# Activation differences of the last 1024 tokens, weight sums and first loads, taken elsewhere in a two-MLP kernel

## The chip, the cores and the metric

The kernel runs on one core of a Trainium2 chip. The metric is the device time in microseconds (us); each version is timed in several runs and the median counts. A core has five engines that run side by side, each working through its own list of instructions in order: TensorE (PE in the profile; matrix products, its weight loads shown as PEld), VectorE (DVE), ScalarE (ACT), GpSimd (POOL) and SyncE (SP), which here only issues DMAs between DRAM and the on-chip memory. An instruction waits for semaphores of the instructions that it depends on, and everything behind it on its engine waits with it.

## The reference

A retention layer, then two MLPs with the same sizes: 3072 tokens, 512 features, 2048 hidden features.

```python
for t in range(S):          # S = 768, 4 batches, 8 heads of 64
    state = gamma * state + outer(k[:, :, t], v[:, :, t])
    y[:, :, t] = scale * q[:, :, t] @ state
x = y.transpose(0, 2, 1, 3).reshape(3072, 512)
h = x @ w_in;   x = (h * cos(h)) @ w_out                       # first MLP, layer 0
h = x @ w_in2;  out = where(h > 0, h, exp(min(h, 0)) - 1) @ w_out2   # second MLP, layer 1
```

## The kernel before

**Number format.** TensorE works on fp32r. Each operand is split into a high part (written by ACT) and a low part (the rest, formed on DVE by a subtraction of two on-chip operands), and each product is the sum of three matmul terms, high-high, high-low, low-high (`PARTS`). A weight tile `w` of a slice holds seven operands of 256 columns in both parts.

**Seven products.** Three of the four MLP products are made as 2 by 2 block products with seven instead of eight multiplications. The weight operands are three blocks of the slice (`a11`, `a12`, `a22`) and four sums (`s1` to `s4`, made of the blocks and of `a21`). The activation operands are four quarters `x0, x1, y0, y1` of a superblock (512 tokens each) and three differences. `A_OF` and `B_OF` name the operands of product `p`; products run in the order 1, 5, 6, 3, 7, 2, 4.

**Stages, in the order in which TensorE runs them** (times of the profile):
- 0 to 31 us: four 128-token units of the retention layer (`scores`, `values`, `update` for unit `n`), with a few dummy matmuls (`warm`). A unit's 1 MB of inputs is one DMA (`load_unit`); `scale_unit` then multiplies q and v by decay factors.
- 31 to 381.7 us, "hidden": `hidden(blk, j)`, the first product of layer 0 without the seven-product form, for six blocks of 512 tokens and eight weight slices `j`, the other 20 units between them. After it come the cosine factor and, for the first two superblocks, the differences (`pair_up`); those of the third are made later, in the next stage (`pair_up_late`, eight times, called from `first_pairs`).
- 381.7 to 614.6 us, "project(0)": `project(0, sb)`, the second product of layer 0 for three superblocks `sb` of 1024 tokens. Each of the 7 x 4 pairs of a superblock is 12 matmuls (line 822) and needs one activation tile `hl`, split by ACT and DVE.
- 614.6 to 890.5 us, "hidden2": the first product of layer 1, 24 steps of (superblock, slice). Step names here are as 2.7 (superblock 2, slice 7). One product is six matmuls (line 628). Steps overlap: `seven(new, old)` interleaves products 1, 5, 6, 3 of the new step with 7, 2, 4 of the old one. Between them DVE must add a saved partial sum to what TensorE has just summed (for instance line 679, between product 7 and product 4 of a step, which sum into the same bank). Then comes the ELU (`elu`: ACT, and DVE lines 724, 733, 736), four subtractions of 128x512 (`differences`) and four stores to DRAM (`put`). At a superblock's first step the seven tiles of the next input (`load_x2`) are loaded and split.
- 890.5 to 1137 us, "project(1)": `project(1, sb)`, the second product of layer 1, with its transposes and stores (`emit`).

**Weights.** They arrive as 8-byte floats. `convert` turns a slice into fp32, forms the four sums (four 128x256 operations), and stores the seven operands to DRAM in two DMAs (three and four operands). `prepare`, called shortly before the slice is needed, loads them back in two DMAs and splits them (ACT, then DVE line 393). `convert` of the slices for project(0) and hidden2 is called in hidden, `prepare` at the end of hidden and in project(0); for the slices of project(1), `convert` is called in hidden2's first two superblocks and `prepare` in its last.

**What sets the order.** The program first lists its operations (`Plan`). TensorE's order is the order of the list. For the other engines `Plan.run` makes the order by list scheduling: a due time for each operation, worked out backwards from TensorE's order and from assumed durations, and then always the ready operation that is due first. An operation marked `ANY` goes to DVE or POOL, whichever comes free first; one that overlaps another on the port is assumed to take `CROWDED` times as long, and a DMA to land after `LANDING`. Buffers come from small pools (11 `c`, 5 `h`, 4 `hl`, 3 `ld`, 8 `w`, 3 `eg`); an operation whose buffer is not free is put off. The outcome is a fixed order of instructions on each engine.

Of the kernel before, what the change touches and what calls it, by code (L numbers as in the profile page):

```python
# [259 lines left out]
def retention_then_two_mlps(ctx: ExitStack, tc: tile.TileContext, attn, tab, weights, out):  # L260
# [117 lines left out]
    def prepare(layer, io, j, lag=0):  # L378
        k = kept[layer, io][j]
        w = Buf("w", [P, NP, 2, Q], F32R)  # L380
        w_t[layer, io, j] = w
        for lo, hi in ((0, 3), (3, NP)):
            t = Buf("c", [P, hi - lo, Q])
            dma(
                hi - lo, lambda t=t: t.t.rearrange("p n q -> p (n q)"),
                lambda lo=lo, hi=hi: k.t[:, lo * Q:hi * Q], [k[lo * Q, hi * Q]], [t], lag,
            )
            high = lambda lo=lo, hi=hi: w.t[:, lo:hi, 0, :]

            turn = -1.0 if layer == 0 else 1.0  # L390
            act(0.1 + 0.26 * (hi - lo), high, lambda t=t: t.t, [t], [w[lo, hi]], lag=lag, scale=turn)
            plan.op("DVE", 0.08 + 0.29 * (hi - lo), lambda t=t, lo=lo, hi=hi, high=high:
                    nc.vector.scalar_tensor_tensor(  # L393
                        out=w.t[:, lo:hi, 1, :], in0=t.t, scalar=turn, in1=high().bitcast(F32),
                        op0=ALU.mult, op1=ALU.subtract,
                    ), [t, w[lo, hi]], [w[lo, hi]], lag)
# [138 lines left out]
    def differences(x, y, u, t4, t4_at, wid, lag):  # L535
# [4 lines left out]
        for o, a, b in todo:  # L540
            tt("ANY", (0.62, 1.2), view(o), view(a), view(b), ALU.subtract, [a, b], [o], lag=lag)


    def hidden(blk, j):
# [40 lines left out]
        else:  # L585
            pair_up(sb, j, g, u, 30)

    def pair_up(sb, j, g, u, lag):
# [4 lines left out]
        put(0, sb, j, 0, 2, lambda: g.t, [g], lag)
        put(0, sb, j, 4, 6, lambda: u.t, [u], lag)
        put(0, sb, j, 6, 7, lambda: t4.t, [t4], lag)

    def pair_up_late(sb, j, lag):
# [430 lines left out]
```

## Time and profile before

| | |
|---|---|
| median of 3 runs | 1138.35 us (1137.36 to 1138.43) |
| the profiled execution | 1138.94 us, its span 1137.2 us |
| TensorE busy | 1081.7 us, 95% of the span |
| DVE, ACT, POOL busy | 858.1, 619.9, 376.2 us |
| DMA | 329.57 MB, 290 GB/s in the mean |

The page gives totals. Three views tell more. The windows give, for chosen stretches, the busy time of each engine, the granted clock of TensorE as a share of full speed (PEclk) and the share of time in which the DMA engines were busy. The waits list whom an engine waited for; a wait below 0.15 us isn't counted. The timeline shows single instructions, with the idle time before an instruction, and what ended it, in square brackets. Six matmuls in one timeline row are one product of hidden2.

### The profile page before, as it was taken

The numbers are of one execution on the slowest core, as the hardware profiler recorded it, in microseconds if no ns is written. First come the engines' busy times: TensorE is split into PE (matmuls) and PEld (weight loads), VectorE is DVE, ScalarE is ACT, GpSimd is POOL, SyncE is SP. The second block draws the span as 40 slices with busy tenths as digits, with TensorE's granted clock in tenths as the row PEclk, the third lists the DMA queues.
The fourth block names the chain that finished last, engine by engine and source line by source line (L and its number), as shares of the span: only waits on it lengthen the run. The fifth ranks groups of instructions, "written<-read, shape, count | busy, mean of one in ns | idle before, by whom it ended". The sixth has DMA issues, their size and how long they took to land. (4 is left out here: it accounts for less than half of the span.)

```text
span 1137.2 us, 14708 instructions
## 1 busy us (share of the span) xinstructions
PE 1081.7 (95%) x5382; PEld 880.8 (77%) x5384; DVE 858.1 (75%) x896; ACT 619.9 (55%) x719; POOL 376.2 (33%) x288
## 2 busy tenths in 40 slices
PE   6999999999999999999998999998988799999997
PEld 4777888888788888877787777776767688888886
DVE  5998999899988847665568898898787845445452
ACT  3564455544567853433446867666677543444442
POOL 2413664466613023222102455675365400000000
PEclk9999999999999999999999999999989899999999
DMA  8776799989999998999998878968878876667661
GB/s 318 288 232 246 274 328 351 340 321 329 341 327 351 328 326 297 354 327 328 338 371 311 301 256 322 335 261 316 291 294 307 296 254 225 218 197 229 203 203 56
DMA packets 117289, 329.57 MB, mean 290 GB/s; under 512 B 8929, under 2 KB 15201, under 8 KB 114273
## 3 DMA queue, kind: packets, MB, share of 16 engines
q1 hardware_dynamic: 117216, 328.64, 81.4%
q8 instruction: 42, 0.69, 0.3%
q14 instruction: 31, 0.25, 0.1%
HBM read 197.01 MB, written 131.60 MB: 289 GB/s over the span
## 5 line engine op out<-in xcount | busy, mean ns | idle before, releaser
L822 PE MATMUL eg<-hl,w 128*128 128x512 f32 x2016 | 465.7, 391 | 2.9 <-DVE hl L293 2.8
L822 PEld LDWEIGHTS eg<-hl,w 128*128 128x128 f32 x2016 | 376.9, 188 | 82.8 <-DVE hl L293 5.0
L293 POOL TENSOR_TENSOR c<-c 128x512 f32<-128x512 f32 (+2 forms) x204 | 283.7, 1398 | 393.0 <-DVE c L293 94.7
L293 DVE TENSOR_TENSOR hl<-ld,hl 128x1024 fp32r<-128x1024 f32 x168 | 218.4, 1313 | 131.3 <-ACT hl L288 131.2
L288 ACT ACTIVATE hl<-ld 128x1024 fp32r<-128x1024 f32 x168 | 176.4, 1059 | 239.4 <-PE eg L822 175.0
L288 ACT ACTIVATE c<-c 128x1024 f32<-128x1024 f32 (+1 forms) x256 | 231.4, 921 | 98.5 <-DVE c L573 65.0
L556 PE MATMUL eg<-hl,w 128*128 128x512 f32 x1152 | 273.9, 394 | 4.4 <-DVE c L578 2.5
L556 PEld LDWEIGHTS eg<-hl,w 128*128 128x128 f32 x1152 | 213.0, 188 | 54.4 <-issue 4.8
L628 PE MATMUL eg<-hl,w 128*128 128x512 f32 x432 | 116.2, 404 | 26.3 <-DVE c L293 22.1
L288 ACT ACTIVATE c<-eg 128x1024 int32<-128x1024 f32 (+2 forms) x96 | 87.5, 911 | 73.5 <-PE eg L556 47.5
L628 PEld LDWEIGHTS eg<-hl,w 128*128 128x128 f32 x432 | 81.4, 193 | 52.0 <-DVE c L293 29.2
L293 DVE TENSOR_TENSOR c<-c 128x512 f32<-128x512 f32 (+2 forms) x72 | 61.4, 854 | 32.5 <-DMA c<-d 21.4
L628 PE MATMUL eg<-ld,w 128*128 128x512 f32 x288 | 74.2, 392 | 3.0 <-ACT h L288 2.9
L293 POOL TENSOR_TENSOR ld<-ld,w 128x512 f32<-128x512 f32 x34 | 47.6, 1414 | 62.5 <-DMA ld<-in_attn 52.5
L628 PEld LDWEIGHTS eg<-ld,w 128*128 128x128 f32 x288 | 54.5, 190 | 15.3 <-ACT h L288 3.3
L393 DVE SCALAR_TENSOR_TENSOR w<-c,w 128x768 fp32r<-128x768 f32 (+1 forms) x48 | 65.4, 1384 | 1.1 <-ACT w L288 1.0
L578 DVE SCALAR_TENSOR_TENSOR c<-c,eg 128x1024 f32<-128x1024 f32 x48 | 58.4, 1216 | 9.1 <-ACT c L288 8.8
L573 DVE SCALAR_TENSOR_TENSOR c<-eg,c 128x1024 f32<-128x1024 f32 x48 | 58.3, 1215 | 5.2 <-ACT c L288 4.6
L288 ACT ACTIVATE w<-c 128x1024 fp32r<-128x1024 f32 (+3 forms) x59 | 52.6, 918 | 16.3 <-DMA c<-d 9.3
L323 DVE SCALAR_TENSOR_TENSOR c<-c 128x512 uint32<-128x512 uint32 x64 | 58.4, 928 | 1.0
L327 DVE SCALAR_TENSOR_TENSOR c<-c 128x512 uint32<-128x512 uint32 x64 | 54.6, 870 | 0.4
L293 DVE TENSOR_TENSOR c<-eg,h 128x512 f32<-128x512 f32 x48 | 32.9, 685 | 19.2 <-PE eg L628 17.9
(50 smaller groups left out, 778.2 us busy)
## 6 DMA issues: line engine op xcount, KB each, us to landing
d<-c SPq DMA_DIRECT2D x197, 512.0 KB, 4.4
ld<-d SPq DMA_DIRECT2D x84, 1024.0 KB, 7.3
c<-d SPq DMA_DIRECT2D x77, 512.0 KB, 5.5
c<-in_weights SPq DMA_DIRECT2D x64, 512.0 KB, 6.1
ld<-in_attn SPq DMA_DIRECT2D x23, 1024.0 KB, 6.8
d<-c SPq DMA_DIRECT2D x24, 384.0 KB, 3.5
c<-d SPq DMA_DIRECT2D x24, 384.0 KB, 5.2
d<-h SPq DMA_DIRECT2D x24, 256.0 KB, 6.9
```

Source lines behind the costliest of these rows:

```text
L288: plan.op("ACT", us, lambda: nc.scalar.activation(out=out_(), in_=in_(), func=func, **kw), r, w, lag)
L293: e.tensor_tensor(out=out_(), in0=a(), in1=b(), op=op)
L323: plan.op("DVE", 0.69, lambda: nc.vector.scalar_tensor_tensor(out=u(), in0=raw.t[:, :, 1], scalar=0x80000000, in1=u(), op0=ALU.bitwise_and ...
L327: plan.op("DVE", 0.69, lambda: nc.vector.scalar_tensor_tensor(out=u(), in0=raw.t[:, :, 0], scalar=29, in1=u(), op0=ALU.logical_shift_right ...
L393: nc.vector.scalar_tensor_tensor(out=w.t[:, lo:hi, 1, :], in0=t.t, scalar=turn, in1=high().bitcast(F32), op0=ALU.mult, op1=ALU.subtract,), ...
L556: nc.tensor.matmul(out=h.t[:, half * TB:(half + 1) * TB], lhsT=quarter(j, qd, wpart, kc % 2), rhs=(xh, xl)[xpart].t[:, kc, :], start=(n == ...
L573: plan.op("DVE", 1.22, lambda: nc.vector.scalar_tensor_tensor(out=g.t, in0=h.t, scalar=1.0 / TWO_PI, in1=n(), op0=ALU.mult, op1=ALU.subtra ...
L578: plan.op("DVE", 1.22, lambda: nc.vector.scalar_tensor_tensor(out=g.t, in0=g.t, scalar=1.0, in1=h.t, op0=ALU.subtract, op1=ALU.mult,), [h, ...
L628: nc.tensor.matmul(out=out_(), lhsT=w.t[:, i, wpart, kc * P:(kc + 1) * P], rhs=x.t[:, xpart, kc, :], start=(start and n == 0), stop=(n == ...
L822: nc.tensor.matmul(out=acc.t[:, i * TB:(i + 1) * TB], lhsT=w[:, A_OF[p], wpart, i * P:(i + 1) * P], rhs=hl.t[:, gpart, k, :], start=(p in ...
```

## The change

Four things change.
1. For superblock 2 of layer 1 (`LATE = 2`), `seven` no longer makes the differences nor stores them. It stores the two activation tiles alone. In project(1), `second_pairs` calls `pair_up_late(1, 2, j)` at two of the four places `jp` of each product of superblock 1, until the eight slices are done: it loads both tiles again, makes the four subtractions and stores what changed.
2. `convert` stores the four blocks of a slice in one DMA and forms no sums. `prepare` loads them in one DMA, forms the four sums itself and splits blocks and sums.
3. Units 1 to 3 are loaded in three DMAs each (`EARLY`) instead of one.
4. Three of the planner's numbers change: `CROWDED`, `LANDING`, and the time assumed for a 128x512 operation on POOL (1.2 to 1.25).

```diff
-CROWDED = 1.4
-LANDING = 2.8
+LATE = 2
+CROWDED = 1.6
+LANDING = 3.0
 ...
     def convert(layer, io, j, lag):
         t = to_f32(layer, io, j, lag)
-        s = Buf("c", [P, WS])
 ...
-        dma(3, lambda: k.t[:, 0:3 * Q], lambda: t.t[:, 0:3 * Q], [t[0, 3 * Q]], [k[0, 3 * Q]], lag)
-        dma(4, lambda: k.t[:, 3 * Q:], lambda: s.t, [s], [k[3 * Q, NP * Q]], lag)
+        k = kept[layer, io][j]
+        dma(4, lambda: k.t, lambda: t.t, [t], [k], lag)
+
+    def prepare(layer, io, j, lag=0):
 ...
+        t, s = Buf("c", [P, WS]), Buf("c", [P, WS])
+        dma(4, lambda: t.t, lambda: k.t, [k], [t], lag)
+        def split(src, at, lo, hi):
 ...
+        split(t, t[0, 3 * Q], 0, 3)
         a11, a12, a22, a21 = ((t, q * Q, q * Q + Q) for q in range(4))
         s1, s2, s3, s4 = ((s, q * Q, q * Q + Q) for q in range(4))
 ...
             tt("ANY", (0.35, 0.7), view(o), view(a), view(b), op, [a, b], [o], lag=lag)
+        split(s, s, 3, NP)
 ...
-            differences(old.x, old.y, old.ux, old.uy, 0, TB, lag)
+            if old.sb < LATE:
+                differences(old.x, old.y, old.ux, old.uy, 0, TB, lag)
             put(1, old.sb, old.j, 2, 4, lambda: old.y.t, [old.y], lag)
             put(1, old.sb, old.j, 0, 2, lambda: old.x.t, [old.x], lag)
-            put(1, old.sb, old.j, 4, 6, lambda: old.ux.t, [old.ux], lag)
-            put(1, old.sb, old.j, 6, 7, lambda: old.uy.t[:, 0:TB], [old.uy[0, TB]], lag)
+            if old.sb < LATE:
+                put(1, old.sb, old.j, 4, 6, lambda: old.ux.t, [old.ux], lag)
+                put(1, old.sb, old.j, 6, 7, lambda: old.uy.t[:, 0:TB], [old.uy[0, TB]], lag)
 ...
+    EARLY = ((0, 1024), (1024, 1536), (1536, 2048))
 ...
-    load_unit(1)
+    load_unit(1, EARLY)
 ...
+    last = [(sb, j) for sb in range(LATE, NSB) for j in range(NJ)]
+    def second_pairs(sb, p, jp):
+        if jp % 3 == 0 and last and last[0][0] == sb + 1:
+            pair_up_late(1, *last.pop(0), 60)
     for sb in range(NSB):
-        project(1, sb, lambda *_: None)
+        project(1, sb, second_pairs)
```

**The order around hidden2's end, VectorE.** The row with L724 (L728 after) is the ELU of step 2.6; `hl<-ld,hl` are low parts of project(1)'s first activations; the first `c<-eg,h` behind them is line 679 (681 after) for step 2.7, on which product 4 of that step waits. Before:

```order
L724 SCALAR_TENSOR_TENSOR c<-c 128x1024
L293 TENSOR_TENSOR hl<-ld,hl 128x1024 x2
L736 SCALAR_TENSOR_TENSOR c<-c 128x512
L293 TENSOR_TENSOR hl<-ld,hl 128x1024
L393 SCALAR_TENSOR_TENSOR w<-c,w 128x3x256
L733 SCALAR_TENSOR_TENSOR c<-c,eg 128x512
L293 TENSOR_TENSOR c<-f,h 128x512
L293 TENSOR_TENSOR c<-eg,h 128x512
```

After:

```order
L728 SCALAR_TENSOR_TENSOR c<-c 128x1024
L383 SCALAR_TENSOR_TENSOR w<-c,w 128x3x256
L295 TENSOR_TENSOR c<-f,h 128x512
L295 TENSOR_TENSOR hl<-ld,hl 128x1024
L295 TENSOR_TENSOR c<-eg,h 128x512
```

Two low parts and the two halves of an ELU no longer stand between that ELU and line 679.

**The order on GpSimd, hidden2 and project(1).** `128x512` are differences, `128x256` weight sums. Before, the last rows of the list:

```order
L293 TENSOR_TENSOR c<-c 128x256 x3
L293 TENSOR_TENSOR c<-c 128x512 x6
L293 TENSOR_TENSOR c<-c 128x256 x2
L293 TENSOR_TENSOR c<-c 128x512 x6
L293 TENSOR_TENSOR c<-c 128x256 x3
L293 TENSOR_TENSOR c<-c 128x512 x5
L293 TENSOR_TENSOR c<-c 128x256 x3
L293 TENSOR_TENSOR c<-c 128x512 x22
```

After, from hidden2's first superblock to the first of the late differences:

```order
L295 TENSOR_TENSOR c<-c 128x256
L295 TENSOR_TENSOR c<-c 128x512 x52
L295 TENSOR_TENSOR c<-c 128x256 x27
L295 TENSOR_TENSOR c<-c 128x512 x3
L295 TENSOR_TENSOR h<-c 128x512
L295 TENSOR_TENSOR c<-c 128x512 x2
L295 TENSOR_TENSOR h<-c 128x512
```

The sums no longer alternate with the differences of the first two superblocks, and in the last superblock GpSimd has 27 sums in place of differences. Of the 32 late differences 19 stand on GpSimd and 13 on VectorE.

**The order at the head of hidden2, VectorE.** `ld<-c,ld` are low parts of hidden2's first input tiles; the second one before, and the last one shown after, is that of product 6, the third that runs. Rows of line 393 (383 after) split weights. Before:

```order
L293 TENSOR_TENSOR hl_4803<-ld_4709,hl_4803 128x1024
L293 TENSOR_TENSOR ld_4810<-c_4770,ld_4810 128x1024
L393 SCALAR_TENSOR_TENSOR w_4827<-c_4619,w_4827 128x3x256
L393 SCALAR_TENSOR_TENSOR w_4827<-c_4622,w_4827 128x4x256
L393 SCALAR_TENSOR_TENSOR w_4833<-c_4690,w_4833 128x3x256
L393 SCALAR_TENSOR_TENSOR w_4833<-c_4693,w_4833 128x4x256
L393 SCALAR_TENSOR_TENSOR w_4872<-c_4789,w_4872 128x3x256
L293 TENSOR_TENSOR ld_4850<-c_4786,ld_4850 128x1024
```

After:

```order
L295 TENSOR_TENSOR hl_4745<-ld_4645,hl_4745 128x1024
L383 SCALAR_TENSOR_TENSOR w_4767<-c_4247,w_4767 128x3x256
L383 SCALAR_TENSOR_TENSOR w_4767<-c_4285,w_4767 128x4x256
L383 SCALAR_TENSOR_TENSOR w_4773<-c_4329,w_4773 128x4x256
L383 SCALAR_TENSOR_TENSOR w_4790<-c_4401,w_4790 128x3x256
L383 SCALAR_TENSOR_TENSOR w_4790<-c_4439,w_4790 128x4x256
L295 TENSOR_TENSOR c_4792<-c_4753,c_4792 128x256
L383 SCALAR_TENSOR_TENSOR w_4810<-c_4753,w_4810 128x3x256
L383 SCALAR_TENSOR_TENSOR w_4773<-c_4289,w_4773 128x3x256
L295 TENSOR_TENSOR ld_4846<-c_4812,ld_4846 128x1024
```

Behind project(0)'s last low part stand one x2 half (product 5) and five splits before, seven splits and a sum after.

## Rows read from the trace of the kernel before

**Rows 1.** Page, busy us (share of the span) xinstructions of each engine.

```profile
PE 1081.7 (95%) x5382; PEld 880.8 (77%) x5384; DVE 858.1 (75%) x896; ACT 619.9 (55%) x719; POOL 376.2 (33%) x288
```

**Rows 2.** Windows: stretch, us; PE, PEld, DVE, ACT, POOL busy (count); PEclk, DMA share, GB/s.

```profile
381.70:614.60 232.90, 230.03 (x1009) 188.82 (x1008) 151.34 (x122) 108.94 (x109) 53.24 (x24) 1.00 0.93 330
614.60:698.60 84.00, 76.00 (x319) 60.20 (x318) 75.37 (x80) 59.88 (x79) 37.43 (x27) 0.98 0.80 292
698.60:782.00 83.40, 78.55 (x338) 62.45 (x336) 75.79 (x86) 58.05 (x80) 55.38 (x42) 1.00 0.81 301
782.00:809.50 27.50, 22.40 (x86) 16.56 (x85) 20.38 (x26) 19.21 (x26) 9.73 (x6) 0.94 0.84 313
809.50:830.60 21.10, 19.64 (x86) 15.62 (x85) 16.48 (x23) 13.39 (x19) 11.75 (x8) 1.00 0.94 339
830.60:890.50 59.90, 47.02 (x188) 37.65 (x187) 49.63 (x52) 40.38 (x52) 34.10 (x21) 0.89 0.82 297
890.50:1130.00 239.50, 239.48 (x1097) 197.74 (x1095) 124.81 (x107) 105.20 (x108) 7.82 (x4) 1.00 0.63 208
```

**Rows 3.** Waits of TensorE: us in total, times, longest.

```profile
PE eg L628 <- DVE c L293: 22.1, 11, 8.5
...
PE eg L822 <- DVE hl L293: 2.8, 3, 1.3
```

**Rows 4.** Timeline of TensorE, hidden2's last steps: start, us, instruction, [idle before].

```profile
834.64 1.52 PE L628 MATMUL eg<-hl,w 128*128 128x512 f32 x6
836.00 1.52 PE L628 MATMUL eg<-ld,w 128*128 128x512 f32 x6
841.21 2.93 PE L628 MATMUL eg<-hl,w 128*128 128x512 f32 x6 [3.68 <-DVE c L293]
...
887.58 2.93 PE L628 MATMUL eg<-hl,w 128*128 128x512 f32 x6 [8.46 <-DVE c L293]
```

**Rows 5.** Timeline of VectorE in the last step.

```profile
875.76 0.69 DVE L293 TENSOR_TENSOR c<-c 128x512 f32<-128x512 f32 x1 [1.20 <-POOL c L293]
876.37 1.22 DVE L724 SCALAR_TENSOR_TENSOR c<-c 128x1024 f32<-128x1024 f32 x1
877.52 4.53 DVE L293 TENSOR_TENSOR hl<-ld,hl 128x1024 fp32r<-128x1024 f32 x2
...
882.58 1.21 DVE L293 TENSOR_TENSOR hl<-ld,hl 128x1024 fp32r<-128x1024 f32 x1
883.71 2.01 DVE L393 SCALAR_TENSOR_TENSOR w<-c,w 128x768 fp32r<-128x768 f32 x1
...
886.85 0.68 DVE L293 TENSOR_TENSOR c<-eg,h 128x512 f32<-128x512 f32 x1
```

**Rows 6.** Timeline of GpSimd in the same stretch.

```profile
876.53 4.44 POOL L293 TENSOR_TENSOR c<-c 128x512 f32<-128x512 f32 x2 [0.81 <-DVE c L293]
```

**Rows 7.** Groups by shape in hidden2: count | busy us, mean ns | idle before.

```profile
L293 POOL TENSOR_TENSOR c<-c 128x512 f32<-128x512 f32 x76 | 120.6, 1587 | 91.9 <-DVE c L724 34.0 <-DVE c L736 29.8 <-issue 14.3
...
L393 DVE SCALAR_TENSOR_TENSOR w<-c,w 128x1024 fp32r<-128x1024 f32 x14 | 21.9, 1562 | 1.0 <-ACT w L288 1.0
...
L393 DVE SCALAR_TENSOR_TENSOR w<-c,w 128x768 fp32r<-128x768 f32 x14 | 19.7, 1411 | 0.1
...
L293 POOL TENSOR_TENSOR c<-c 128x256 f32<-128x256 f32 x25 | 25.3, 1026 | 23.4 <-DVE c L327 17.8 <-ACT c L288 4.9 <-DVE c L293 0.4
```

**Rows 8.** The same groups in project(0): low parts of the activations.

```profile
L293 DVE TENSOR_TENSOR hl<-ld,hl 128x1024 fp32r<-128x1024 f32 x82 | 109.2, 1356 | 42.5 <-ACT hl L288 42.4
```

**Rows 9.** The same groups in project(1).

```profile
L293 DVE TENSOR_TENSOR hl<-ld,hl 128x1024 fp32r<-128x1024 f32 x81 | 100.5, 1241 | 88.8 <-ACT hl L288 88.8
```

**Rows 10.** Timeline of TensorE at the first step of the last superblock.

```profile
788.75 2.50 PE L628 MATMUL f<-ld,w 128*128 128x512 f32 x5 [2.65 <-DVE ld L293]
```

**Rows 11.** Timeline of TensorE at the head of hidden2.

```profile
620.37 2.04 PE L628 MATMUL eg<-ld,w 128*128 128x512 f32 x6 [2.87 <-ACT h L288]
```

**Rows 12.** Timeline of TensorE in the first units.

```profile
11.35 1.09 PE L489 MATMUL f<-w,ld 128*64 128x128 f32 x16 [2.48 <-DVE ld L293]
```

More of the change, by code (lines that the diff above doesn't have):

```diff
@@ L358, in retention_then_two_mlps @@
     kept = {
-        (layer, io): [dram_buf([P, NP * Q]) for _ in range(NJ)] for layer, io in ((0, 1), (1, 0), (1, 1))
+        (layer, io): [dram_buf([P, WS]) for _ in range(NJ)] for layer, io in ((0, 1), (1, 0), (1, 1))
     }
@@ L364, in convert @@
         t = to_f32(layer, io, j, lag)
-        s = Buf("c", [P, WS])
+        k = kept[layer, io][j]
+        dma(4, lambda: k.t, lambda: t.t, [t], [k], lag)
+    def prepare(layer, io, j, lag=0):
+        k = kept[layer, io][j]
+        w = Buf("w", [P, NP, 2, Q], F32R)
+        w_t[layer, io, j] = w
+        t, s = Buf("c", [P, WS]), Buf("c", [P, WS])
+        dma(4, lambda: t.t, lambda: k.t, [k], [t], lag)
+        turn = -1.0 if layer == 0 else 1.0
+        def split(src, at, lo, hi):
+            view = lambda: src.t[:, 0:(hi - lo) * Q].rearrange("p (n q) -> p n q", q=Q)
+            high = lambda: w.t[:, lo:hi, 0, :]
+            act(0.1 + 0.26 * (hi - lo), high, view, [at], [w[lo, hi]], lag=lag, scale=turn)
+            plan.op("DVE", 0.08 + 0.29 * (hi - lo), lambda: nc.vector.scalar_tensor_tensor(
+                out=w.t[:, lo:hi, 1, :], in0=view(), scalar=turn, in1=high().bitcast(F32),
+                op0=ALU.mult, op1=ALU.subtract,
+            ), [at, w[lo, hi]], [w[lo, hi]], lag)
+        split(t, t[0, 3 * Q], 0, 3)
         a11, a12, a22, a21 = ((t, q * Q, q * Q + Q) for q in range(4))
@@ L373, in convert @@
             tt("ANY", (0.35, 0.7), view(o), view(a), view(b), op, [a, b], [o], lag=lag)
-        k = kept[layer, io][j]
-        dma(3, lambda: k.t[:, 0:3 * Q], lambda: t.t[:, 0:3 * Q], [t[0, 3 * Q]], [k[0, 3 * Q]], lag)
-        dma(4, lambda: k.t[:, 3 * Q:], lambda: s.t, [s], [k[3 * Q, NP * Q]], lag)
[L378 to L396, printed above, removed]
+        split(s, s, 3, NP)
     cst = Buf("w", [P, NP * 2 * Q])
@@ L540, in differences @@
         for o, a, b in todo:
[L541 removed]
+            tt("ANY", (0.62, 1.25), view(o), view(a), view(b), ALU.subtract, [a, b], [o], lag=lag)
     def hidden(blk, j):
@@ L585, in hidden, with pair_up, pair_up_late @@
         else:
-            pair_up(sb, j, g, u, 30)
-    def pair_up(sb, j, g, u, lag):
+            pair_up(0, sb, j, g, u, 30)
+    def pair_up(layer, sb, j, g, u, lag):
         y = Buf("c", [P, 2 * TB])
         t4 = Buf("h", [P, TB])
-        dma(4, lambda: y.t, lambda: gd[0, sb].t[:, j, 2:4, :], [gd[0, sb][j * NP + 2, j * NP + 4]], [y], lag)
+        dma(4, lambda: y.t, lambda: gd[layer, sb].t[:, j, 2:4, :],
+            [gd[layer, sb][j * NP + 2, j * NP + 4]], [y], lag)
         differences(g, y, u, t4, 0, TB, lag)
[L593 to L597, printed above, removed]
+        put(layer, sb, j, 0, 2, lambda: g.t, [g], lag)
+        put(layer, sb, j, 4, 6, lambda: u.t, [u], lag)
+        put(layer, sb, j, 6, 7, lambda: t4.t, [t4], lag)
+    def pair_up_late(layer, sb, j, lag):
         g = Buf("c", [P, 2 * TB])
         u = Buf("c", [P, 2 * TB])
-        dma(4, lambda: g.t, lambda: gd[0, sb].t[:, j, 0:2, :], [gd[0, sb][j * NP, j * NP + 2]], [g], lag)
-        pair_up(sb, j, g, u, lag)
+        dma(4, lambda: g.t, lambda: gd[layer, sb].t[:, j, 0:2, :], [gd[layer, sb][j * NP, j * NP + 2]], [g], lag)
+        pair_up(layer, sb, j, g, u, lag)
     x2d = [dram_buf([P, NP, 2 * TB]) for _ in range(NSB)]
@@ L906, in retention_then_two_mlps @@
     update(0)
-    load_unit(2)
+    load_unit(2, EARLY)
     scale_unit(2)
@@ L913, in retention_then_two_mlps @@
     update(1)
-    load_unit(3)
+    load_unit(3, EARLY)
     scale_unit(3)
@@ L958, in first_pairs @@
         if jp == 3 and p in (5, 3, 7, 4) and later and sb < 2:
-            pair_up_late(NSB - 1, later.pop(0), 60)
+            pair_up_late(0, NSB - 1, later.pop(0), 60)
         if sb == NSB - 1 and p == 4:
```

4 lines of the change are left out of this document (2 added, 2 removed).

## The prediction

> **What bounds the kernel now.** Read the page first: TensorE is busy for 95% of the span [rows 1], so time can only be saved where it waits or runs slowly. The windows by stage come next [rows 2]. Project(1) is 239.50 us with 239.48 us of TensorE: nothing to win there, only to lose. Project(0) loses about 3 us. Hidden2, between 614.6 and 890.5 us, is where the loss is. To size it I need the time of a product that waits for nothing: consecutive ones start 1.36 us apart (834.64 and 836.00) [rows 4]. Superblock 0 has 53 products in its window (its first step has only four), so 72.1 us of work in 84.0 us: 11.9 us lost. Superblock 1 has 56: 76.2 in 83.4, 7.2 us lost. Of the last superblock, the first two steps (14 products, 19.0 us) take 27.5, 8.5 us lost; the next two take 21.1, 2.1 us lost; the remaining four and the last three products (31, so 42.2 us) take 59.9, 17.7 us lost. Together 47.4 us.
>
> Who is waited for: the longest entry of the waits is line 628 on a VectorE operation `c`, 22.1 us in 11 waits, the longest 8.5 us [rows 3]. The timeline puts two of them at 841.21 and 887.58, with 3.68 and 8.46 us of idle time, and the product behind each takes 2.93 instead of 1.52 us [rows 4]: the granted clock of that window is 0.89 [rows 2], so part of it ran at the lower of TensorE's levels, 1.2 instead of 2.4 GHz, after the engine had sat idle. A wait is paid nearly twice over its end.
>
> Why 8.46 us: TensorE needs line 679 of step 2.7, and VectorE comes to it at 886.85 only [rows 5]. Ahead of it, from 876.37 on, stand an ELU, three low parts of project(1)'s activations, weight splits and smaller pieces. Two of the low parts take 4.53 us, the third 1.21 [rows 5]; beside the first two GpSimd runs two differences, 4.44 us [rows 6]. So VectorE is both queued wrongly and slowed by GpSimd.
>
> **The change part by part** (sum against the profiled execution, 1138.94 us, which is 0.6 above the median).
>
> *End of hidden2.* The 32 differences of the last superblock leave it: 1.587 us each on GpSimd [rows 7], 50.8 us. In come 32 weight sums, 27 on GpSimd by the order, 1.026 us each [rows 7]: 27.7 us. GpSimd has 23 us less to do there, and the sums of the slices converted in the last steps are gone too. In the new order, line 681 of step 2.7 stands behind the ELU, one three-wide split, a small sum of 0.68 us and one low part: 1.22 + 1.41 + 0.68 + 1.24 + 0.68 = 5.2 us [rows 5, 7, 9] against 11.2 us (876.37 to 887.53) now. Counted from the same start it would be done at 881.6, and TensorE has been waiting since 879.1 (887.58 less 8.46) [rows 4]: 2.5 us of wait left at most, and less if the ELU comes earlier, which stands behind GpSimd's differences today (0.69 us operation at 875.76 with 1.20 us idle before) [rows 5]. For the wait of 3.68 us (step 2.3) no queue of that kind is left: in the new order two half ELUs and one split are the most that stands between a step's product 7 and its sum, about 3 us against the 4.1 us (three times 1.36) that three other products cover. So of 17.7 us I leave 2.7: gain 15. Bounds: 17.7 if nothing waits; 13.7 if the 31 products lose what those of superblock 1 lose (7.2 / 56 each, 4.0).
>
> *Head of the last superblock* (8.5 us lost, one of its waits 2.65 us on an x2 half [rows 10]). The seven x2 halves still come in a bunch, and in the new order line 681 of step 1.7 stands behind three of them. I take +1, between -4 and +4.
>
> *Head of hidden2.* Sums of the first slices are now made there. Product 6 of step 0.0 waits 2.87 us today [rows 11]. In front of its low part VectorE has two splits and one small sum more and one x2 half less: 1.41 + 1.56 + about 1.0 - 1.4 = 2.6 us [rows 7]. I take +2.5, between 0 (if TensorE waits for the loads there anyway) and +6 (the next halves are late too).
>
> *Rest of superblocks 0 and 1.* 32 sums and three of seven stored operands of each slice for project(1) leave this stretch, in which 19.1 us are lost, some 14 of them not at the head. The sums ran on GpSimd at 1.026 us each [rows 7] and held the differences up. I take -2, between -6 and +3, since the whole order is new.
>
> *Project(1).* 32 late differences, 16 loads and 24 stores move in; the stores were in hidden2 before, the loads (512 KB each, 8.4 MB) are new. DMA has room: 0.63 busy there, 0.93 in project(0) [rows 2]. The eight late slices of layer 0 are made in project(0) in just this way, and it shows the price: 53.24 us of GpSimd and 2.8 us of waits for `hl` [rows 2, 3], the low part at 1.356 instead of 1.241 us [rows 8, 9]. 19 differences on GpSimd are 30.2 us [rows 7]; by proportion 1.6 us. Bounds 0 and +5.
>
> *Start.* With units loaded in pieces and unit 0's v no longer behind unit 1's megabyte, the wait of 2.48 us at 11.35 [rows 12] should mostly go, but VectorE is busy for nearly all of the time that follows. I take -1.5, between -2.5 and 0.
>
> *End of hidden, project(0).* 32 sums now stand before project(0) instead of in hidden's middle; the DMA traffic falls (24 slices, six 128 KB operands less each, 18.9 MB). TensorE waits little on either side today. +0.5, between -2 and +4.
>
> Sum: -15 + 1 + 2.5 - 2 + 1.6 - 1.5 + 0.5 = -12.9, so 1126.0 for the profiled execution and 1125.5 for the median.
>
> A rule of the Trainium skill bears on where the differences go. The rows say that two low parts beside two differences took 4.53 us, and alone 1.24 each [rows 5, 6, 9]. SBUF — State Buffer, section Who interferes with whom, says that a VectorE instruction with two on-chip inputs and a GpSimd instruction that reads on-chip memory exclude each other for the whole instruction. The trace agrees in kind. By the rule taken alone a difference on GpSimd costs as much in project(1) as in hidden2, and the sum would end at the third rival's 1154 us; by the rows of project(0) it ends at 1125.5.
>
> **The rivals.**
> 1. *The waits move to the heads.* The tail is gained, but the bunches of x2 halves cost the upper bounds (+4, +6), and superblocks 0 and 1 give nothing: -15 + 4 + 6 + 1.6 + 0.5 = -2.9, so 1135.5. For it: both heads are VectorE queues that the change makes longer. Against it: GpSimd is emptier.
> 2. *All of it is gained*: 17.7 + 4 at the head + 3 in superblocks 0 and 1 + 2.5 at the start, less 1.6: -25, so 1113. Against it: 25 us would be over half of the loss in hidden2, by an order that still has the same VectorE work.
> 3. *Slower, by GpSimd in project(1).* Each of the 19 differences there locks VectorE out for its 1.587 us, and TensorE, which has no slack in this stage, waits for the low parts: 30.2 instead of 1.6 us, 1138.4 - 12.9 + 28.6 = 1154. It decides when VectorE's time for one pair exceeds TensorE's 12 matmuls, twice 1.36 or 2.72 us; a low part beside GpSimd took 2.27 (half of 4.53) [rows 5], so it would need something more in the same pair. Half of it already makes the kernel slower than before. Against it stands project(0).
> 4. *No change*: the differences are late again wherever they go. The order shows that they do move, so little is left for this.
>
> **How the numbers follow.** My forecast (1116 to 1131) 0.68, rival 1 (1131 to 1136) 0.16, rival 2 (below 1116) 0.07, rival 3 0.06, rival 4 0.03. The range reaches from 1115, which leaves out most of rival 2, to 1135, which takes in most of rival 1. A measurement here tells about 0.2%, 2.3 us, from no change. Faster by more (below 1136.1): 0.90; within: 0.04; slower: 0.06.
>
> **What would show it.** Right: the waits of line 628 on VectorE's `c` fall from 22.1 us [rows 3] to below 10, the wait at step 2.7 is below 3 us and the clock in the window of the last four steps is 0.97 or more; GpSimd is busy for some 30 us more in project(1) and TensorE stays at 98% there. Wrong: a wait of 4 us or more at product 6 of step 0.0 or at product 4 of step 1.7 (rival 1); several microseconds of waits for `hl` at project(1)'s first two superblocks (rival 3); new waits in hidden, whose order I have not priced beyond 4 us.

## The result and the profile after

| | before | after |
|---|---|---|
| median of 4 runs each, us | 1137.86 (1136.33 to 1138.43) | 1118.40 (1117.68 to 1123.21) |
| ratio | | 0.984, 95% interval 0.981 to 0.987 |
| profiled execution, its span, us | 1138.94, 1137.2 | 1118.94, 1117.2 |

The kernel is 19.5 us faster; the prediction said 12.9, and its range held the time. One execution of the kernel with parts 1 and 2 took 2449.62 us, marked slow, and is left out of its median and range below; counted in, it makes that median the 1117.5 us that two expectations name.

The first page of after answers to [rows 1]: TensorE's and VectorE's work is nearly the same, GpSimd's 35 us more.

```profile
PE 1077.8 (96%) x5382; PEld 880.8 (79%) x5384; DVE 857.9 (77%) x884; ACT 620.9 (56%) x719; POOL 411.6 (37%) x300
```

The windows by stage, laid over the same places of the program as [rows 2] (project(0), superblocks 0 and 1 of hidden2, steps 2.0 and 2.1, steps 2.2 and 2.3, the rest of hidden2, project(1); columns as there):

```profile
378.60:607.10 228.50, 228.50 (x1010) 189.27 (x1009) 158.15 (x121) 109.99 (x108) 67.42 (x33) 1.00 0.86 307
607.10:690.90 83.80, 76.14 (x320) 60.41 (x319) 75.05 (x70) 59.50 (x79) 61.48 (x41) 0.96 0.68 251
690.90:774.70 83.80, 78.51 (x338) 62.35 (x337) 70.88 (x84) 58.07 (x80) 45.36 (x29) 1.00 0.81 296
774.70:804.20 29.50, 23.24 (x85) 17.55 (x84) 24.50 (x29) 18.68 (x25) 14.29 (x11) 0.83 0.75 276
804.20:823.50 19.30, 19.30 (x86) 15.71 (x85) 17.80 (x23) 16.77 (x24) 5.81 (x6) 1.00 0.80 286
823.50:868.60 45.10, 43.08 (x188) 34.71 (x187) 37.32 (x45) 35.47 (x46) 20.58 (x19) 1.00 0.66 236
868.60:1108.00 239.40, 237.25 (x1089) 196.04 (x1088) 140.15 (x124) 107.10 (x110) 33.19 (x18) 1.00 0.80 279
```

The last row of hidden2 is where the time went: 45.1 instead of 59.9 us, the clock 1.00 instead of 0.89. The row of steps 2.0 and 2.1 is the reverse: 29.5 instead of 27.5 us, the clock 0.83 instead of 0.94. In project(1), whose last 7 and 9 us both windows leave out, TensorE goes from 239.48 busy of 239.50 us to 237.25 of 239.40, with 25 us more of GpSimd and the DMA engines busy for 0.80 instead of 0.63; the whole stage is 1.8 us longer (the thirds in the table below).

The waits of TensorE say who is still late ([rows 3] has 22.1 us in its first line):

```profile
PE eg L630 <- DVE c L295: 11.7, 9, 3.5
PE eg L630 <- DVE ld L295: 6.5, 3, 3.2
...
PE f L766 <- DVE c L295: 2.1, 1, 2.1
```

The timeline of TensorE at four places: product 6 of step 0.0 (two rows, 1.63 and 3.15 us of waiting), product 4 of step 1.7, product 4 of step 2.7 (0.78 us where [rows 4] has 8.46), and one transposing piece in project(1).

```profile
611.58 0.49 PE L630 MATMUL eg<-ld,w 128*128 128x512 f32 x1 [1.63 <-ACT ld L290]
615.23 1.22 PE L630 MATMUL eg<-ld,w 128*128 128x512 f32 x2 [3.15 <-DVE ld L295]
...
788.40 2.93 PE L630 MATMUL eg<-hl,w 128*128 128x512 f32 x6 [3.50 <-DVE c L295]
...
867.05 1.66 PE L630 MATMUL eg<-hl,w 128*128 128x512 f32 x6 [0.78 <-DVE c L295]
...
1008.99 0.63 PE L766 MATMUL f<-ident,c 128*128 128x128 f32 x4 [2.15 <-DVE c L295]
```

On VectorE, line 681's sum of step 2.7 (the row at 866.30) has one low part ahead of it and waits for TensorE rather than TensorE for it (the queue of before is in [rows 5]):

```profile
863.97 0.68 DVE L295 TENSOR_TENSOR c<-f,h 128x512 f32<-128x512 f32 x1
864.68 1.23 DVE L295 TENSOR_TENSOR hl<-ld,hl 128x1024 fp32r<-128x1024 f32 x1
866.30 0.69 DVE L295 TENSOR_TENSOR c<-eg,h 128x512 f32<-128x512 f32 x1 [0.40 <-PE eg L630]
```

### The profile page after: what moved, and what is told of

The parts are those of the page before. It is cut to its first block, busy times and chain, and to the rows that moved or that the text cites. A ratio compares the mean times of both kernels' runs of the same rounds, so it can differ in the third digit from the quotient of the medians.

```text
span 1117.2 us, 14628 instructions
## 1 busy us (share of the span) xinstructions
PE 1077.8 (96%) x5382; PEld 880.8 (79%) x5384; DVE 857.9 (77%) x884; ACT 620.9 (56%) x719; POOL 411.6 (37%) x300
## 2 busy tenths in 40 slices
DMA packets 114695, 323.27 MB, mean 289 GB/s; under 512 B 8640, under 2 KB 14912, under 8 KB 112064
## 5 line engine op out<-in xcount | busy, mean ns | idle before, releaser
L295 POOL TENSOR_TENSOR c<-c 128x512 f32<-128x512 f32 (+2 forms) x207 | 305.3, 1486 | 382.6 <-DMA c<-d 138.1
L295 DVE TENSOR_TENSOR hl<-ld,hl 128x1024 fp32r<-128x1024 f32 x168 | 227.7, 1365 | 110.1 <-ACT hl L290 109.7
L630 PE MATMUL eg<-hl,w 128*128 128x512 f32 x432 | 113.3, 398 | 12.5 <-DVE c L295 11.7
L295 DVE TENSOR_TENSOR c<-c 128x512 f32<-128x512 f32 (+2 forms) x61 | 49.5, 813 | 31.7 <-DMA c<-d 24.7
L295 POOL TENSOR_TENSOR ld<-ld,w 128x512 f32<-128x512 f32 x32 | 44.3, 1397 | 72.1 <-DMA ld<-in_attn 58.8
L295 POOL TENSOR_TENSOR h<-c 128x512 f32<-128x512 f32 x22 | 36.4, 1654 | 60.2 <-DMA d<-h 46.5
```

The lines of the kernel that those rows point to most:

```text
L295: e.tensor_tensor(out=out_(), in0=a(), in1=b(), op=op)
L630: nc.tensor.matmul(out=out_(), lhsT=w.t[:, i, wpart, kc * P:(kc + 1) * P], rhs=x.t[:, xpart, kc, :], start=(start and n == 0), stop=(n == ...
```

## The experiments

All ratios are to the kernel before, run on the same chip. The stage lengths below are measured from the start of a stage's first product to that of the next stage's, in one profiled execution each (us; TensorE's waits in brackets). "Heads" are the steps in which a superblock of hidden2 begins. "From superblock 1" and "from step 1.5" say where the late differences begin in the last three rows.

```
                        hidden  project(0)  0.0-0.1      0.2-0.7     1.0-1.7     2.0-2.1     2.2 to end    project(1) thirds
before                  350.7   232.9       20.0 (2.9)   64.0 (5.1)  83.3 (4.9)  27.5 (5.1)  80.8 (14.3)   79.5  80.0  87.4
after                   345.0   228.5       24.4 (6.2)   59.4 (1.5)  83.8 (5.3)  29.6 (6.3)  64.3 (2.0)    79.1  82.4  87.2
part 1 alone            350.7   230.6       18.7 (2.8)   64.0 (5.1)  83.4 (4.8)  27.1 (4.7)  62.7 (0.9)    79.1  80.0  87.1
part 2 alone            347.5   228.5       24.5 (6.9)   65.2 (5.0)  80.4 (2.7)  23.2 (1.8)  86.8 (21.1)   79.5  80.0  87.1
part 3 alone            347.9   230.0       21.5 (3.8)   63.9 (5.0)  83.4 (4.9)  27.6 (5.1)  80.9 (14.3)   79.6  80.0  87.2
part 4 alone            346.7   228.7       17.6 (1.8)   61.3 (2.7)  96.7 (11.9) 34.0 (9.8)  75.9 (10.6)   80.6  80.0  87.3
no subtractions         352.7   228.5       18.7 (2.9)   63.8 (4.9)  84.2 (4.2)  27.1 (4.7)  72.7 (9.1)    80.3  80.0  87.1
part 1 + GpSimd load    349.6   229.6       19.4 (2.6)   65.3 (4.8)  84.3 (4.2)  27.1 (4.6)  64.4 (1.9)    80.2  82.9  87.1
parts 1 and 2           348.8   229.3       23.9 (6.6)   66.8 (6.6)  80.5 (2.6)  21.6 (1.9)  64.7 (2.1)    79.1  80.3  87.1
parts 1 to 3            346.1   228.5       24.7 (6.9)   65.2 (5.0)  80.4 (2.7)  23.0 (1.8)  65.6 (3.0)    79.1  80.6  87.2
all late on GpSimd      344.9   228.5       24.4 (5.9)   59.4 (1.5)  84.0 (4.1)  29.6 (6.5)  64.1 (1.9)    79.1  80.0  87.2
1, from superblock 1    353.3   229.4       21.3 (4.2)   65.4 (4.9)  80.0 (2.3)  19.5 (0.2)  66.8 (3.7)    86.5 104.5  87.1
1 and 2, from sb. 1     349.0   230.2       24.5 (6.9)   65.2 (5.0)  85.1 (5.8)  19.1 (0.0)  64.9 (2.2)    87.7 101.2  87.1
1, from step 1.5        351.5   228.5       17.5 (2.1)   65.4 (4.8)  82.4 (3.6)  19.1 (0.0)  62.4 (0.8)    83.0  92.4  87.0
```

### Each part alone

Part 1 is `LATE`, the `if`s, and `second_pairs`; part 2 is the new `convert` and `prepare`; part 3 is

```diff
-    load_unit(1)
+    load_unit(1, EARLY)
```

(for units 1 to 3); part 4 is the planner's numbers.

> The kernel before with part 1 of the change alone: the last superblock's differences made in project(1). The order up to hidden2's last superblock is that of before. Theory (the differences hold VectorE, GpSimd and buffers there): the 17.7 us lost from 830.6 us to hidden2's end fall to 6 or less, project(1) grows by 1 to 3 us, total 9 to 14 us faster than before. Rival (the gain came from the order being made anew with other numbers): less than 4 us faster.

> The kernel before with part 2 alone: weight sums formed when slices are prepared, fewer and larger stores. Theory: hidden and project(0) gain the 3 to 5 us that the full change gained there, the head of hidden2 loses 2 to 5 us, hidden2's end keeps most of its loss (10 us or more of 17.7); total within 4 us of before. Rival (the sums are what held hidden2's end up): 8 us or more faster, the loss at the end below 8 us.

> The kernel before with part 3 alone: units 1 to 3 loaded in three pieces each. Theory: the first wait for unit 0's v (2.48 us) goes, but line 556 starts no earlier than 30 us, since VectorE and the loads of units 3 and 4 set that; total within 3 us of before. Rival (the pieces shorten the start as I had predicted): line 556 starts at 29.5 us or earlier and the total is 1.5 us faster or more.

> The kernel before with part 4 alone: the planner's three numbers. Theory: no operation changes, the order does; hidden2's end keeps 12 us or more of its 17.7 us loss; total within 4 us of before. Rival (the new order is what gained): 8 us or more faster, with project(0) at 229 us and no wait for hl there.

Measured: part 1 1117.26 us, ratio 0.9834 (0.9814 to 0.9855); part 2 1.0015 (1.0002 to 1.0028); part 3 1.0001 (0.998 to 1.0021); part 4 1.0058 (1.0037 to 1.008). Part 1 is the whole gain: 19.6 us, more than the 9 to 14 expected, and 18.1 us of it lie between step 2.2 and the end of hidden2; project(1) did not grow as expected. Its window from step 2.4 to the end, against 59.90 us [rows 2]:

```profile
825.80:869.10 43.30, 42.52 (x188) 34.86 (x187) 37.29 (x47) 38.25 (x50) 5.03 (x4) 1.00 0.84 298
```

Part 2 gains in superblock 1 and at the head of superblock 2 and loses it at the head of hidden2 and at its end, where its wait at step 2.7 is 13.31 us:

```profile
832.96 2.93 PE L627 MATMUL eg<-hl,w 128*128 128x512 f32 x6 [5.71 <-DVE c L293]
...
883.35 2.93 PE L627 MATMUL eg<-hl,w 128*128 128x512 f32 x6 [13.31 <-DVE c L293]
```

Part 4 re-makes the whole order and still has the late sum at step 2.7; so a new order as such is not the cure. It made the kernel 5.4 us slower, where within 4 was expected.

```profile
890.83 2.93 PE L628 MATMUL eg<-hl,w 128*128 128x512 f32 x6 [6.72 <-DVE c L293]
```

### What part 1 took away

Why did VectorE come late to line 679's sum of step 2.7? By the planner's own account, when product 3 of that step ends nine of the eleven `c` tiles are held, eight of them by the activations and differences of steps 2.5 and 2.6, which wait for GpSimd's subtractions and for their stores. Line 679's neighbour (line 715, a row ahead) writes the first half of the same new tile, and line 679 can't be placed before line 715 has taken that tile. In part 1 alone six tiles are held. Theory "held tiles": both sums are put off for want of a tile, and the list fills VectorE with low parts and splits. A rival within the planner is rank: line 715's sum is due later than that other work, whatever tiles are free. The rival on the chip is the port: 32 subtractions on GpSimd slow VectorE down. Two kernels take either the subtractions or the stores with their held tiles away and leave the other. The first:

```diff
-            differences(old.x, old.y, old.ux, old.uy, 0, TB, lag)
+            if old.sb < NSB - 1:
+                differences(old.x, old.y, old.ux, old.uy, 0, TB, lag)
```

> The kernel before with the 32 subtractions of the last superblock in hidden2 left out (that part of the result is not computed); its stores stay, so the activation tiles and the difference tiles are held until the stores as before, and the order still has three low parts of project(1) ahead of line 679's sum for step 2.7. Theory 'held tiles' (the sum comes late because the 11 `c` tiles are full of operands that wait to be stored, so the order puts other VectorE work ahead of it): the stretch from step 2.4 to the end of hidden2 stays above 55 us (59.7 before) with a TensorE wait of 8 us or more at step 2.7; 1128 to 1137 us in all. Rival 'GpSimd beside VectorE' (32 subtractions, 50.8 us of GpSimd, slow VectorE down): the stretch falls to 43 to 46 us, the total to 1117 to 1121.

Measured: 1127.34 us (1125.98 to 1129.53), 0.9929 (0.9904 to 0.9955). The window from step 2.4 to the end, TensorE there, and VectorE's queue ahead of the sum (the last row's first instruction is the sum of step 2.7):

```profile
824.60:877.90 53.30, 44.30 (x188) 35.62 (x187) 40.29 (x48) 39.78 (x51) 5.32 (x4) 0.93 0.97 348
```

```profile
875.15 2.93 PE L628 MATMUL eg<-hl,w 128*128 128x512 f32 x6 [8.98 <-DVE c L293]
```

```profile
864.58 1.23 DVE L293 TENSOR_TENSOR hl<-ld,hl 128x1024 fp32r<-128x1024 f32 x1 [1.01 <-ACT hl L288]
866.01 2.51 DVE L293 TENSOR_TENSOR hl<-ld,hl 128x1024 fp32r<-128x1024 f32 x2 [0.21 <-ACT hl L288]
868.43 2.09 DVE L393 SCALAR_TENSOR_TENSOR w<-c,w 128x768 fp32r<-128x768 f32 x2
870.44 0.68 DVE L734 SCALAR_TENSOR_TENSOR c<-c,eg 128x512 f32<-128x512 f32 x1
...
873.81 1.28 DVE L293 TENSOR_TENSOR c<-eg,h 128x512 f32<-128x512 f32 x2
```

GpSimd is busy for 5.32 us in the whole window (34.10 in [rows 2]), each low part takes its 1.23 us, and the wait of 8.98 us is there all the same: at step 2.7 it is the queue, not the port. The stretch came out at 53.3 us, below the 55 that was named, and the total a little below its range, so the rival has its share too: the wait of 3.68 us at step 2.3 [rows 4] is gone. The second kernel is part 1 with GpSimd loaded by operations that hold no `c` tile:

```diff
+                for _ in range(8):
+                    extra = plan.op("POOL", 0.001, lambda: nc.gpsimd.tensor_tensor(
+                        out=ident, in0=ident, in1=ident, op=ALU.mult), [ident_b], [ident_b])
+                    plan.ops[extra][3].add(done4)
```

> Part 1 alone (1117.3 us), with eight GpSimd operations of 128x128 with two on-chip inputs put into each of the last superblock's eight steps behind product 4: some 6 us a step, as much as the four differences (4 x 1.587 us) that part 1 took away; they hold no `c` tile. Theory 'held tiles': the stretch from step 2.4 to the end of hidden2 stays below 47 us (43.3 in part 1 alone), 1116 to 1121 us in all. Rival 'GpSimd beside VectorE': the stretch returns to 52 to 60 us, the total to 1127 to 1135.

Measured: 1119.82 us (1116.24 to 1123.27), 0.9858 (0.9812 to 0.9905). Window from 2.4 on, GpSimd's added operations, and TensorE at step 2.7:

```profile
827.40:871.30 43.90, 43.04 (x187) 34.60 (x186) 37.15 (x45) 37.29 (x49) 30.88 (x44) 1.00 0.88 306
```

```profile
L717 POOL TENSOR_TENSOR ident<-ident 128x128 f32<-128x128 f32 x40 | 28.0, 700 | 3.1
```

```profile
869.82 1.67 PE L631 MATMUL eg<-hl,w 128*128 128x512 f32 x6 [0.79 <-DVE c L295]
```

With 30.9 us of GpSimd, nearly the 34.1 of before, the stretch is 43.9 us. One reservation: these operations are 0.70 us long, the subtractions 1.59, so one of them can hold VectorE up for less. From step 2.2 to the end of hidden2 the kernel takes 80.8 us before, 72.7 without the subtractions and 62.7 when their stores are gone too. So 8.1 us go with the subtractions (their time on GpSimd and the tiles that waited for them) and 10.0 with the stores and what they held. The shares hang on the order in which the two are taken away: GpSimd loaded anew costs 1.7 us (64.4 against 62.7), not 8.1.

What put the sum late in the list is less sure than the two runs make it look. The planner can be run with one thing altered; the orders that it gives were not run on the chip, and its times are its own. In the kernel before, line 715's sum of step 2.7 is due at 855.1 by the planner, and the low parts, the split and the ELUs that go first at 808 to 820. Allowing this sum a tile whatever is free changes no row. A due time 45 us earlier places it 8.6 us earlier, with the tiles as they are, and the wait planned at step 2.7 falls from 7.7 to 0.8 us (20 or 30 us earlier change no row, since that still leaves it behind the others). Line 679's sum is due at 808.2, but nothing passes this on to line 715, which must take the tile first. So there it is rank. In the kernel without the subtractions it is mostly tiles: allowing the sum a tile takes the planned wait from 9.0 to 0, an earlier due time only to 6.6. Tiles count before as well, by other rows: with twelve instead of eleven the planner makes an order that waits 0.9 us. And in the changed kernel ten are held at the same moment, yet the sum is placed 0.7 us later, since nothing due earlier could be placed then. The runs show that part 1 brings the sum forward in VectorE's list and what that gains; whether rank or tiles held it back in the kernel before, no run shows.

### Parts 1 and 2, parts 1 to 3

> Parts 1 and 2 (late differences and the sums at the split), without the pieces and without the new numbers. If the gains of the two add up by stage (part 1 alone: 1117.3; part 2 alone is 2.5 us shorter in hidden, 2.9 in superblock 1 and 4.3 at the head of superblock 2, and 4.5 longer at the head of hidden2 and 6.1 at its end, where part 1 takes the held tiles away): 1110 to 1115 us. If the sums at the end of hidden2 hold tiles as the differences did: the stretch from 2.4 on is above 50 us and the total 1120 or more. If nothing of part 2 stays: 1116 to 1119.

> The changed kernel with the numbers of before in the planner (parts 1, 2 and 3). If the new numbers do in the whole what they do alone (part 4 alone: superblock 1 longer by 13.4 us, 1.0058 of before): 1108 to 1113 us. If their effect alone was that order's accident: 1115 to 1120 us, as parts 1 and 2 (1117.5).

Measured: 1115.61 us (1115.32 to 1119.36), 0.9832 (0.9784 to 0.9879); and 1118.65 us (1113.96 to 1123.97), 0.984 (0.9801 to 0.9879). Neither differs from part 1 alone or from the changed kernel. Part 2's gain does not add to part 1's. What part 2 costs at hidden2's end goes with part 1 (64.7 against 86.8 us), as "held tiles" has it, though not it alone; its gains of 2.9 and 5.5 us in superblock 1 and its successor's head are paid back at the head of hidden2 (5.2) and in steps 0.2 to 0.7 (2.8). The new numbers, which alone cost 13.4 us in superblock 1 and 6.5 at the next head, cost 3.4 and 6.5 there in the whole (the changed kernel against parts 1 to 3) and give 5.8 back in steps 0.2 to 0.7; the two medians are the same.

### GpSimd in project(1)

All late differences on GpSimd (the program's `ANY` becomes `POOL` for them):

> The changed kernel with all 32 late differences in project(1) on GpSimd (19 there now, 13 on VectorE). Third rival of the prediction (each difference locks VectorE out for its 1.587 us, TensorE waits for the low parts): 13 more make project(1) some 20 us longer, 1130 us or more. Forecast by proportion: project(1) has room on VectorE, its waits stay below 5 us, 1117 to 1122 us.

Measured: 1115.85 us (1114.53 to 1117.01), 0.9826 (0.9781 to 0.9871), slightly below the range expected and, with parts 1 and 2, the lowest median, though its interval overlaps that of the changed kernel. Window of project(1), and two groups in it:

```profile
866.60:1105.80 239.20, 239.20 (x1097) 197.62 (x1095) 135.31 (x111) 107.00 (x110) 52.90 (x31) 1.00 0.82 280
```

```profile
L295 DVE TENSOR_TENSOR hl<-ld,hl 128x1024 fp32r<-128x1024 f32 x83 | 110.5, 1334 | 79.1 <-ACT hl L290 79.0
L295 POOL TENSOR_TENSOR c<-c 128x512 f32<-128x512 f32 x23 | 40.9, 1779 | 82.7 <-DMA c<-d 67.0 <-issue 13.4 <-ACT hl L290 1.5
```

TensorE is busy for 239.20 of 239.20 us: the third rival falls. The mean low part rises from 1.241 [rows 9] to 1.334 us; those 19 that ran beside GpSimd for 0.4 us or more took 1.71 us in the mean (1.23 to 2.35), the others 1.22. The Trainium skill, SBUF — State Buffer, section Who interferes with whom, says that a VectorE instruction with two on-chip inputs contends with a GpSimd instruction that reads on-chip memory. The single low part agrees with that. It costs TensorE nothing here; the likely reason is that VectorE works for 135 of 239 us only and low parts are made ahead.

### How much more can be taken late

"Held tiles" should also explain the head of the last superblock, where superblock 1's differences hold the tiles.

```diff
-LATE = 2
+LATE = 1
```

> Part 1 alone, with the differences of superblock 1 late as well as those of superblock 2 (LATE = 1). Theory 'held tiles': what delays the x2 halves and line 679's sums at the end of superblock 1 is the same as at the end of hidden2, so the head of the last superblock (steps 2.0 and 2.1: 27.1 us in part 1 alone, 4.65 of waits; the wait of 3.04 us on an x2 half at step 2.0) falls to 20 to 24 us and superblock 1 (83.4) by 1 to 4 us; project(1), with 64 differences, loses 2 to 6 us: 1109 to 1117 us in all. Rival 'that head waits for its loads, whatever holds tiles': steps 2.0 and 2.1 stay at 26 to 28 us, and project(1) makes it 1118 to 1123 us.

> Parts 1 and 2 with the differences of superblocks 1 and 2 late. Against parts 1 and 2 with superblock 2 late (1117.5 us; the head of the last superblock is 21.6 us there already): 'held tiles' gives another 1 to 4 us in superblock 1 and its end, project(1) takes 0 to 6: 1113 to 1120 us.

Measured: 1139.3 us (1135.0 to 1146.04), 1.0019 (0.9998 to 1.004); with part 2 1146.63 us, 1.0084 (1.0064 to 1.0104). The head did fall, from 27.1 to 19.5 us (19.1 with part 2), 14 products with next to no wait; as at hidden2's end, that doesn't tell the tiles from the rest of what was taken away. With part 2, superblock 1 got longer (85.1 against 80.5 us) instead of shorter. And project(1) took 31.8 us more (29.4 with part 2). Its first two thirds in part 1 alone and then with `LATE = 1`:

```profile
869.10:948.20 79.10, 79.10 (x362) 65.33 (x361) 58.06 (x54) 40.41 (x42) 13.02 (x7) 1.00 0.95 330
948.20:1028.20 80.00, 80.00 (x369) 66.20 (x368) 47.76 (x38) 35.32 (x36) 19.84 (x13) 1.00 0.97 348
```

```profile
865.90:952.40 86.50, 80.66 (x362) 66.49 (x361) 59.79 (x52) 38.56 (x41) 29.34 (x16) 0.98 0.94 330
952.40:1056.90 104.50, 87.55 (x370) 70.78 (x369) 59.95 (x52) 35.07 (x36) 24.83 (x16) 0.90 0.97 347
```

The DMA share is the same 0.94 to 0.97 at the same 330 to 348 GB/s, over a longer time: the DMA engines were nearly full already in part 1 alone. Neither expectation had that. The last run tried to take only as much as seemed to fit:

```diff
-LATE = 2
+LATE = [(1, j) for j in range(5, 8)] + [(2, j) for j in range(8)]
...
-        if jp % 3 == 0 and last and last[0][0] == sb + 1:
+        if jp % 3 == 0 and (sb or p in (3, 7)) and last and last[0][0] == sb + 1:
```

> Part 1 alone (1117.3 us), with the differences of superblock 1's last three steps (1.5 to 1.7) taken late as well. 'Held tiles': as with all eight of superblock 1 late, steps 2.0 and 2.1 fall from 27.1 to 19 to 21 us and superblock 1 from 83.4 to 80 to 82. The price: 2.36 MB more of DMA in project(1) for each of the three slices, 7.1 MB or 20.5 us at the 345 GB/s that the DMA engines reached there; in part 1 alone they were 0.94 and 0.88 busy in the two thirds in question, which leaves some 15 us; eight slices more cost 32 us of project(1). If the price is the bytes beyond that room: project(1) is 0 to 6 us longer, 1106 to 1114 us in all. Rival 'any difference of superblock 1 holds project(1) up' (its second third waits for the operand whatever the bytes): 8 us or more, 1117 to 1125 us.

Measured: 1123.28 us (1116.53 to 1128.72), 0.9879 (0.9848 to 0.9911). The head fell to 19.1 us as expected; project(1) grew by 16.1 us instead of 0 to 6, which is the rival's range. The second third's window, then the timeline of TensorE with the largest wait and that of VectorE with what stood before the total (the last row) on which TensorE waits:

```profile
941.10:1033.60 92.50, 82.08 (x370) 67.38 (x369) 57.19 (x52) 35.54 (x36) 15.41 (x11) 0.94 0.92 332
```

```profile
1010.94 1.09 PE L767 MATMUL f<-ident,c 128*128 128x128 f32 x4 [8.89 <-DVE c L295]
```

```profile
994.91 0.69 DVE L295 TENSOR_TENSOR c<-c 128x512 f32<-128x512 f32 x1 [2.68 <-DMA c<-d]
...
1001.25 0.69 DVE L295 TENSOR_TENSOR c<-c 128x512 f32<-128x512 f32 x1 [2.29 <-DMA c<-d]
...
1006.44 2.36 DVE L295 TENSOR_TENSOR c<-c 128x512 f32<-128x512 f32 x2 [2.04 <-DMA c<-d]
...
1009.56 1.23 DVE L295 TENSOR_TENSOR c<-eg,c 128x1024 f32<-128x1024 f32 x1
```

VectorE stands at late differences whose loads have not landed, 2.0 to 2.7 us each, and TensorE's total stands behind them. VectorE's waits for such loads in this third, here and in part 1 alone:

```profile
DVE c L295 <- DMA c<-d: 13.6, 6, 2.7
```

```profile
DVE c L295 <- DMA c<-d: 2.6, 1, 2.6
```

The room of 15 us that the expectation counted wasn't there: its 0.88 was of a window that reached into the last third, and with the 0.95 and 0.97 above some 6 us are left, an estimate by which 14 of the 20.5 us remain as a price. But full DMA engines are not what this run shows: their share is 0.92 in this third, and the loads for which VectorE stood here landed 6.4 to 9.0 us after they were issued, against a median of 10.2 us for such loads in part 1 alone, where TensorE had no wait. So the place of the late differences in VectorE's list, ahead of the total, has its part, and how the 16.1 us divide stays open. With all differences on GpSimd the queue behind the loads would be another engine's; the wait of 2.15 us in the changed kernel did vanish that way (second third 80.0 instead of 82.4 us), but for slices of superblock 1 it wasn't tried. No version was found that beats the changed kernel by more than the measurement tells.

## Why the prediction was right, point by point

| term of the sum, us | forecast | after less before | part 1 alone less before |
|---|---|---|---|
| end of hidden2 (2.2 to end) | -15 | -16.5 | -18.1 |
| head of last superblock | +1 | +2.0 | -0.4 |
| head of hidden2 | +2.5 | +4.5 | -1.3 |
| rest of superblocks 0, 1 | -2 | -4.2 | 0.0 |
| project(1) | +1.6 | +1.8 | -0.7 |
| start | -1.5 | +2.6 | +0.8 |
| hidden | in the next | -5.7 | +0.1 |
| project(0) | +0.5 | -4.5 | -2.3 |
| sum | -12.9 | -20.0 | -21.9 |

The columns of differences are of two profiled spans.

- **End of hidden2.** Place, sign and size held: 0.78 us of wait at step 2.7 where below 3 was said, the clock at 1.00. It was the term that carries the result. The reason given was a queue of low parts and GpSimd beside it. The queue is shown; the slowing by GpSimd is not what made the wait at step 2.7 (8.98 us without the subtractions). Why the queue was there the prediction did not ask; the runs put 8.1 us on the subtractions and 10.0 on the stores and what they held, and leave rank against tiles open. Line 630's waits on `c` are 11.7 us, not below 10.
- **Heads.** The first rival's sign came: product 6 of step 0.0 waits 4.78 us (1.63 and 3.15), above the 4 that was named, and product 4 of step 1.7 waits 3.50, below it. The two heads cost 6.5 us, not 3.5, and the rest of both superblocks gave 4.2 back instead of 2. The first cost comes with part 2 (24.5 us there alone), the second with part 4: parts 1 to 3 without it take 23.0 us at the second head.
- **Start.** The sign was wrong. The wait of 2.48 us [rows 12] did shrink, to 0.57, but others took its place (1.99 us before unit 0's `update`, 1.39 for unit 4's scale). Part 3 alone is no gain either (32.1 against 31.0 us). The same order of instructions took 33.6 us in the changed kernel and 31.8 in the run with all late differences on GpSimd, so about 2 us of this term are not the change's. Most of it lies in the clock: from 14 to 22 us TensorE was granted 0.58 in the changed kernel's profile and 1.00 in the other, and the same 16 matmuls took 1.98 and 1.09 us:

```profile
16.49 1.98 PE L490 MATMUL f<-w,ld 128*64 128x128 f32 x16 [0.94 <-ACT w L290]
```

```profile
16.27 1.09 PE L490 MATMUL f<-w,ld 128*64 128x128 f32 x16 [0.94 <-ACT w L290]
```

- **Hidden and project(0).** I had given them +0.5, and they fell by 10.2 us. For project(0) the change is not shown to be the cause: the kernel without the subtractions has the same order as before up to superblock 1 and took 228.5 us there, against 232.9 in the profile of before. That profile's 2.8 us of waits for `hl` [rows 3], from which I priced project(1), belong largely to that execution: in two others with this order up to there they are 0 and 1.1 us. In hidden, parts 2, 3 and 4 each alone are 2.7 to 4.0 us shorter than before, and the kernel with before's order isn't; so that gain comes with the new orders. Which row of them gives it, I did not settle.
- **Project(1).** +1.8 for +1.6, but by another road: the waits were not for `hl` but one of 2.15 us for a total on VectorE. GpSimd is 25 us busier, not 30. What I took for the price (GpSimd) costs nothing, and what I called room (DMA, 0.63 in the mean of the stage) is nearly used up in the thirds in which the work must be done, 0.95 to 0.97. The count of bytes was short too: the eight slices' `x0` and `x1` are now stored twice, 4.2 MB more, so that the DMA moves 323.27 MB, 6.3 less than before, where 18.9 less and 8.4 more were counted.
- **Sum.** The profiles are 7.1 us better than the forecast, the medians 6.6: 10.7 by hidden and project(0), 2.2 by the rest of superblocks 0 and 1 and 1.5 by the end, against 4.1 lost at the start, 3.0 at the heads and 0.2 in project(1). So the total came nearer than its terms, and that is luck: the errors arise in different stages and only happen to offset one another in part. Part 1 alone gives 19.6 us, the whole change 19.5: parts 2 to 4 add nothing to it that can be measured.

## What to carry to other kernels

When an instruction on which the bound engine waits stands late in another engine's list, ask what kept it from being placed earlier, its rank or a buffer that was not free, and alter each by itself: here the planner's order took no notice of a due time 30 us earlier and gave way to one 45 us earlier. Work with no reader nearby can be moved out as a whole, and together with its stores that gave more (18.1 us) than leaving out the work alone (8.1). Before moving it, count the bytes in the stretch in which it must now be done, not in the mean of the stage; and work that waits for loads may be better off the engine that the bound engine waits for (one wait of 2.15 us went that way here).

## What the hardware showed unexpectedly

The same list of instructions took 228.5 and 232.9 us in project(0), and 31.8 and 33.6 us in the start, in different executions (the latter at a granted clock of 1.00 and 0.58 between 14 and 22 us): a term of a few microseconds can't be read from one profile of each kernel. And 31 GpSimd operations in project(1), 52.9 us, cost TensorE nothing, although the low parts that met them took 1.71 instead of 1.22 us.
